# A sparse-attention and channel-mix kernel whose score matmuls write to PSUM in another order, with a re-ordered start

## Chip, cores and metric

The kernel runs on one core of one Trainium2 chip. The metric is the device time of one execution in microseconds. The kernel before took 571.46 us (median of three runs, 569.92 to 574.84).

## What is computed

Attention over 4 batches, 8 heads, 768 positions and a head size of 64. Positions lie in 24 blocks of 32. A query sees its own block and the neighbours, the first and the last block, and three sampled blocks; queries of the first and last block see everything. The attention's result is the input x of a channel mix with a gate:

```python
scores = scale * np.matmul(q, k.transpose(0, 1, 3, 2))
# mask: |blk_i - blk_j| <= 1, first and last block, sampled_blocks[qb]
attn = softmax(where(mask, scores, -1e9));  x = attn @ v     # as (B, S, 512)
x_prev = x shifted by one position
xk = mu_k * x + (1.0 - mu_k) * x_prev
xr = mu_r * x + (1.0 - mu_r) * x_prev
k = np.maximum(xk @ w_k, 0.0)
out = sigmoid(xr @ w_r) * (k * k @ w_v)
```

The weights arrive as 64-bit floats; q, k and v are 32-bit.

## The kernel before

**Attention** runs in 26 units (`all_units`, L266). Units 0 to 3 are wide: the first and last query block of one batch, against all 768 keys. Units 4 to 25 are near: one query block n = 1 to 22 of all four batches, against eight key blocks: three neighbours, the last or first block, and the block's own slots with the sampled blocks. A near unit (`near_unit`, L542) does two groups of head pairs. For each, 16 fp32 matmuls of 256 columns (L559) write scores `s`, DVE takes the maximum (L567), four exponentials on ACT write `p` (L539 in `direct_exp`), eight PE transposes and two copies turn it to `pt` (L523, L527 or L529), and 32 matmuls with the values give `o` (L585). `finish` (L648) divides, transposes (`tx`) and stores into `xt`.

A key slot holds values as (slot, head pair, position). The score matmul of L559 reads eight slots and writes them one after the other, so that a row of `s` is (c, slot, position). The values of a block of four slots lie in the partitions as (position, slot), so `p` has to be in the order (c, position, slot): L574 reads `s` as it lies, and the function `turned` (L576) writes `p` with a step of four values.

**The channel mix** goes over 12 tiles of 256 positions (`mixer`, L837): `split_x` makes xk and xr with their high and low parts (differences on POOL L740, mix on DVE L743, high part on ACT L750, low part on POOL L752), `gate` does r = xr w_r (L776), `hidden` h = xk w_k, relu and square (L794 to L811), `values` the product with w_v (L823). Each product is three matmuls: high-high, high-low, low-high.

**Weights** come in 20 blocks of 128 x 512 (`weight`, L358): blocks 0 to 3 are w_r, 4 to 11 w_k, 12 to 19 w_v. A block is 512 KB of 64-bit floats. ACT scales the upper words into `wmag` (L373), three DVE instructions make a 32-bit float `wf` (L378, L382, L386), then the high part is a copy (L396 on POOL for the blocks in `HI_POOL`, else L398 on ACT) and POOL subtracts it for the low part (L400). Blocks 0 to 11 are loaded into eight places of `early_w`, the others into `raw` tiles, which share four buffers with `p`.

**The sampled blocks** are looked up on the chip: `mask_setup` (L302) loads their numbers and a table of what is seen anyway, and `pack` (L310 to L336, 20 DVE instructions on one partition) replaces doubles by an empty block and packs six numbers into one word. SP reads that word before it issues the loads of sampled keys (L488) and values (L505) of each near unit.

**Order.** `plan.add(engine, ns, rank, ...)` lists every step with a cost and a due time (rank, in us). `Plan.order` (L190) goes through a model of the engines and picks for each engine, among the steps that can start soon, the one due first; the result is the fixed order of every engine's instructions. Costs and due times thus only set orders; the tables of due times stand at the end (L890 to L911). Each engine takes its instructions strictly in that order, and SP issues all loads and stores on one queue.

## Time and profile before

| | |
|---|---|
| runs | 571.46 us median (569.92, 571.46, 574.84) |
| profiled execution, its own time | 571.98 us |
| its span, first to last instruction | 570.2 us |
| mean granted clock of TensorE | 0.987 |
| busy: PE, ACT, POOL, DVE | 537.7, 325.2, 291.0, 269.6 us |
| bytes by DMA | 86.09 MB |
| chain that ended last, share of PE | 80% |

A row of the profile names the source line, engine, operation, output and input tile and the count; then busy time and the mean of one, and the idle time of the engine just before such instructions with what ended it. `<-` in a bracket names the instruction or transfer that was waited for. PE is the matmul stream and PEld its weight loads, which overlap it. An fp32 matmul counts as two matmul instructions with a weight load each, a transpose or a matmul of the mix as one. In the chain of waits a row is start, length, what, and how many instructions.

### The profile page before, as it was taken

The page shows a single profiled execution, that of the slowest core. Times are in us where ns is not written, and L with a number is a line of the kernel's source. Part 1 is how long each engine was busy: PE and PEld are TensorE (multiplying, and loading weights), DVE is VectorE, ACT ScalarE, POOL GpSimd, SP SyncE. Part 2 cuts the span into 40 slices and gives each one's busy share as a digit, 9 for nine tenths or more (in the row PEclk, how much of TensorE's full clock was granted, in tenths as well). Part 3 has the DMA queues.
Part 4 walks back from the last instruction along what each step waited for, and adds up shares of the span by engine and source line. Part 5 has one row for each costly group of instructions (what it writes and reads, how often), then busy time and mean ns, then how long its engine had stood idle before and what let it go on. Part 6 is the DMA issues. An engine that isn't in the chain of part 4 may idle for free.

```text
span 570.2 us, 18311 instructions
## 1 busy us (share of the span) xinstructions
PE 537.7 (94%) x7724; PEld 438.5 (77%) x7724; DVE 269.6 (47%) x533; ACT 325.2 (57%) x612; POOL 291.0 (51%) x359
## 2 busy tenths in 40 slices
PE   6788778979999999999999999999999999999997
PEld 2454556856887798897798798887877989889886
DVE  0877998887445353434424524433452242142411
ACT  0676687768478468467464756546564356424330
POOL 0430456887266066346066285373383663448752
PEclk9799899999999999999999999999999999999999
DMA  8999899773653553362651804135510302110001
GB/s 314 395 398 342 295 343 352 260 228 94 192 182 95 172 164 116 112 189 76 189 167 29 278 24 157 36 100 166 169 39 20 95 19 84 32 39 1 20 20 38
DMA packets 34183, 86.09 MB, mean 151 GB/s; under 512 B 5010, under 2 KB 5780, under 8 KB 31124
## 3 DMA queue, kind: packets, MB, share of 16 engines
q1 hardware_dynamic: 34100, 84.92, 44.5%
q8 instruction: 61, 1.00, 0.7%
q14 instruction: 22, 0.18, 0.1%
HBM read 78.60 MB, written 6.29 MB: 149 GB/s over the span
## 4 chain that ended last, share of the span: by engine, by line
PE 80%; DVE 9%; DMA 4%; ACT 2%; POOL 2%; issue 2%; SPq 0%; DVEq 0%; ACTq 0%
PE v L823 23%; PE o L585 6%; PE s L559 6%; PE t L523 6%; PE r_0p L776 5%; PE h_1p L794 5%; PE h_3p L794 5%; PE h_0p L794 5%; PE h_2p L794 5%; PE r_1p L776 4%; PE tw L523 2%; PE sw L608 2%; DVE nm L567 2%; PE tx L668 2%; DMA raw<-w_v 1%
## 5 line engine op out<-in xcount | busy, mean ns | idle before, releaser
L823 PE MATMUL v<-wv,k 128*128 128x512 f32 (+1 forms) x600 | 145.0, 391 | 0.0
L823 PEld LDWEIGHTS v<-wv,k 128*128 128x128 f32 x600 | 106.8, 188 | 22.8 <-DVE x L661 0.8
L539 ACT ACTIVATE p<-s,nm 128x256 f32<-128x256 f32 x176 | 104.1, 728 | 18.1 <-DVE nm L569 13.8
L567 DVE TENSOR_REDUCE nm<-s 128x4 f32<-128x1024 f32 x44 | 53.6, 1219 | 16.1 <-PE s L559 16.1
L523 PE MATMUL t<-ident,p 128*128 128x128 f32 x352 | 54.6, 278 | 4.7 <-ACT z L783 2.4
L585 PE MATMUL o<-VA,pt 128*32 128x65 f32 x2816 | 49.9, 222 | 6.7 <-ACT pt L527 4.0
L585 PEld LDWEIGHTS o<-VA,pt 128*32 128x32 f32 x2816 | 42.3, 109 | 16.9 <-issue 9.7
L752 POOL TENSOR_TENSOR xr<-xr_1f,xr 128x256 fp32r<-128x256 f32 x24 | 17.7, 737 | 70.8 <-ACT xr L750 70.8
L523 PEld LDWEIGHTS t<-ident,p 128*128 128x128 f32 x352 | 40.2, 140 | 16.1 <-ACT z L783 2.9
L527 ACT COPY pt<-t 128x512 f32<-128x512 f32 x68 | 40.7, 604 | 18.7 <-PE t L523 15.7
L559 PE MATMUL s<-KA,q 64*32 64x256 f32 x1408 | 46.5, 387 | 1.6 <-DVE wf L386 1.2
L743 DVE SCALAR_TENSOR_TENSOR xr_1f<-xr_1d,mk,xt 128x128 f32<-128x128 f32 x48 | 17.9, 372 | 55.9 <-POOL xr L752 46.3
L831 DVE SCALAR_TENSOR_TENSOR z<-v,z 128x512 f32<-128x512 f32 (+1 forms) x25 | 16.8, 670 | 50.1 <-PE v L823 50.0
L685 ACT COPY xt<-tx 128x512 f32<-128x512 f32 x22 | 13.0, 591 | 42.1 <-PE tx L668 42.0
L794 PE MATMUL h_0p<-xk,wk 128*128 128x256 f32 x288 | 37.0, 282 | 0.0
L776 PE MATMUL r_1p<-wr,xr 128*128 128x512 f32 x144 | 36.4, 400 | 0.6 <-ACT h_3k L807 0.6
L794 PE MATMUL h_3p<-xk,wk 128*128 128x256 f32 x288 | 36.4, 281 | 0.0
L743 DVE SCALAR_TENSOR_TENSOR xr_0f<-xr_0d,mk,xt 128x128 f32<-128x128 f32 x48 | 20.3, 424 | 34.0 <-POOL xk L752 13.9
L776 PE MATMUL r_0p<-wr,xr 128*128 128x512 f32 x144 | 36.4, 400 | 0.0
L794 PE MATMUL h_1p<-xk,wk 128*128 128x256 f32 x288 | 36.3, 281 | 0.0
L794 PE MATMUL h_2p<-xk,wk 128*128 128x256 f32 x288 | 36.3, 280 | 0.0
L794 PEld LDWEIGHTS h_0p<-xk,wk 128*128 128x128 f32 x288 | 35.1, 188 | 0.7
(139 smaller groups left out, 940.1 us busy)
## 6 DMA issues: line engine op xcount, KB each, us to landing
VA<-vt SPq DMA_DIRECT2D x93, 260.0 KB, 3.8
KA<-kt SPq DMA_DIRECT2D x90, 256.0 KB, 3.7
VA<-vw SPq DMA_DIRECT2D x24, 260.0 KB, 6.1
KA<-kq SPq DMA_DIRECT2D x16, 384.0 KB, 6.7
out<-z SPq DMA_DIRECT2D x23, 256.0 KB, 2.2
q<-qt SPq DMA_DIRECT2D x22, 256.0 KB, 4.3
early_w<-w_k SPq DMA_DIRECT2D x8, 512.0 KB, 6.4
raw<-w_v SPq DMA_DIRECT2D x8, 512.0 KB, 5.0
```

The costliest lines, as they stand in the source:

```text
L523: nc.tensor.transpose(tp.ap[:, i, :], p.ap[:, x : x + P], ident.ap)
L527: plan.add(ACT, 200 + 0.75 * P * many, rank + 0.1, lambda: nc.scalar.copy(pt.ap[:, 0:many], tp.ap[:, 0:many]), reads=[(tp,)], writes=[(pt,)])
L539: plan.add(ACT, 262 + 0.83 * width, rank, lambda: nc.scalar.activation(turned(p.ap[:, out]), view(), AF.Exp, bias=nm(), scale=SCALE), read ...
L559: nc.tensor.matmul(s.ap[ROWS[j], row, a * 256 : (a + 1) * 256].rearrange("p (n x) -> p n x", x=BLK), q.ap[half, (hp * QB + j) * BLK : (hp ...
L567: nc.vector.tensor_reduce(out=nm.ap.rearrange("p (r a) -> p r a", r=2), in_=s.ap.rearrange("p r (a x) -> p r a x", a=2), axis=AX.X, op=ALU ...
L585: nc.tensor.matmul(o[gi].ap[ROWS[j], i * DV : (i + 1) * DV], pts[row].ap[:, 2 * a + g, ROWS[j]], VA.ap[:, c0 + g, j, h * DV : (h + 1) * DV ...
L743: nc.vector.scalar_tensor_tensor(out=parts(f.ap[:, i, :]), in0=parts(d.ap), scalar=mk.ap[:, which, c : c + 1], in1=cols(c, 1), op0=ALU.mul ...
L752: plan.add(POOL, 80 + 2.4 * MIX * tw, rank + O_MIX, lambda f=f, cs=cs: nc.gpsimd.tensor_tensor(out=dst.ap[:, 1, cs], in0=f.ap, in1=dst.ap[ ...
L776: nc.tensor.matmul(pr.ap[:, 0:512], xr.ap[:, a, c, :], wr.ap[:, w, c, :], start=(c == 0 and m == 0), stop=(c == CC - 1 and m == 2))
L794: nc.tensor.matmul(ph.ap[:, ff * TT : (ff + 1) * TT], wk.ap[:, w, c, f * P : (f + 1) * P], xk.ap[:, a, c, :], start=(c == 0 and m == 0), s ...
L823: nc.tensor.matmul(pv.ap[:, 0:width], k2.ap[:, a, f, i * P : (i + 1) * P], wv.ap[:, w, f, cs], start=(f == 0 and m == 0), stop=(f == FC - ...
L831: plan.add(DVE, 150 + 1.05 * width, done, lambda pv=pv, cs=cs: nc.vector.scalar_tensor_tensor(out=z.ap[:, cs], in0=pv.ap[:, 0:width], scal ...
```

## The change

Four edits, and new tables of due times:

1. The score matmul writes its 256 columns in the order (c, position, slot), by a stepped output, and reads its eight key slots as before. `s` then lies as `p` has to, and the exponentials read and write 256 values that follow each other.
2. The due time of the sampled blocks' loads and of `pack` is -300 in place of -10.9 and -7.9, so both come first.
3. `HI_POOL` is 0 to 11 in place of 0 to 19: the high parts of the eight w_v blocks are copied on ACT (L398).
4. The planner's costs of `pack`, two weight instructions and the differences on POOL are changed.

```diff
-        plan.add(DVE, 4000, PICK + 3, pack, reads=[(number,), (con,)], writes=[(r,), (e,), (packed,)])
+        plan.add(DVE, 5500, PICK, pack, reads=[(number,), (con,)], writes=[(r,), (e,), (packed,)])
...
-            plan.add(DVE, 500, rank, shift, reads=[(mag,)], writes=[(mag,)])
+            plan.add(DVE, 600, rank, shift, reads=[(mag,)], writes=[(mag,)])
...
-            plan.add(DVE, 800, rank, tail, reads=[(mag,), (raw,)], writes=[(f,)])
+            plan.add(DVE, 930, rank, tail, reads=[(mag,), (raw,)], writes=[(f,)])
...
-    def direct_exp(p, out, s, view, nm, rank, key, turned=lambda x: x):
+    def direct_exp(p, out, s, view, nm, rank, key):
...
-            turned(p.ap[:, out]), view(), AF.Exp, bias=nm(), scale=SCALE), reads=[(s,), key[0]], writes=[(p, key[1])], table="exp")
+            p.ap[:, out], view(), AF.Exp, bias=nm(), scale=SCALE), reads=[(s,), key[0]], writes=[(p, key[1])], table="exp")
...
-                                s.ap[ROWS[j], row, a * 256 : (a + 1) * 256].rearrange("p (n x) -> p n x", x=BLK),
+                                s.ap[ROWS[j], row, a * 256 : (a + 1) * 256].rearrange("p (c x t) -> p c t x", c=2, t=QB),
...
-                                K[half, first : first + 2 * QB, j, xs], start=True, stop=True, skip_group_check=True)
+                                K[half, first : first + 2 * QB, j, xs].rearrange("p (c t) x -> p c t x", c=2), start=True, stop=True, skip_group_check=True)
...
-                direct_exp(p, slice(i * 256, (i + 1) * 256), s, lambda s=s, row=row, a=a: s.ap[:, row, a * 256 : (a + 1) * 256].rearrange("p (c j x) -> p c j x", c=2, j=QB),
-                           lambda nm=nm, i=i: nm.ap[:, i : i + 1], t1 + O_EXP[kind], ((nm,), i),
-                           lambda one: one.rearrange("p (c x j) -> p c j x", c=2, j=QB))
+                direct_exp(p, slice(i * 256, (i + 1) * 256), s, lambda s=s, row=row, a=a: s.ap[:, row, a * 256 : (a + 1) * 256],
+                           lambda nm=nm, i=i: nm.ap[:, i : i + 1], t1 + O_EXP[kind], ((nm,), i))
...
-        engine, ns, sub = (DVE, 70 + 1.04 * tw, nc.vector) if dve else (POOL, 80 + 2.07 * tw, nc.gpsimd)
+        engine, ns, sub = (DVE, 70 + 1.04 * tw, nc.vector) if dve else (POOL, 280 + 1.9 * tw, nc.gpsimd)
...
-HI_POOL = frozenset(range(20))
-
-PICK = -10.949
+HI_POOL = frozenset(range(12))
+
+PICK = -300.0
...
-UNIT_AT = [-9.20, 11.48, 39.66, 33.10, 52.53, 63.60, 71.98, 78.76, 95.46, 104.84, 132.94, 141.83, 159.00, 167.89, 184.38, 195.98, 213.06, 224.21, 284.51, 310.70, 320.53, 331.75, 388.52, 435.25, 445.15, 471.93]
+UNIT_AT = [-22.18, -27.40, -7.23, -18.64, 4.45, 12.07, 20.72, 26.61, 52.69, 67.00, 123.73, 130.36, 138.82, 146.33, 178.75, 187.42, 201.49, 212.32, 220.90, 269.30, 284.47, 293.08, 299.62, 341.83, 351.51, 457.85]
...
```

One line falls away above L576, so lines behind it have a number less by one in the changed kernel. Three places show how the instructions move.

**SP's queue at the start of the program.** `early_w` is a weight block, `q` a unit's queries, KA keys and VA values of the wide units; `number` and `con` are the two loads of the search. Before:

```order
L364 DMA early_w<-w_r 128x1024
L364 DMA early_w<-w_k 128x1024 x3
L461 DMA q_105<-qt 128x256
L467 DMA KA<-kq 128x768 x2
L461 DMA q_109<-qt 128x256
L467 DMA KA<-kq 128x768 x2
L364 DMA early_w<-w_r 128x1024
L471 DMA VA<-vw 128x520 x6
L467 DMA KA<-kq 128x768 x4
L471 DMA VA<-vw 128x520 x4
L461 DMA q_187<-qt 128x256
L471 DMA VA<-vw 128x520 x2
```

And now:

```order
L364 DMA early_w<-w_r 128x1024
L364 DMA early_w<-w_k 128x1024
L307 DMA number<-blocks 1x144
L308 DMA con<-seen 1x462
L364 DMA early_w<-w_k 128x1024 x2
L364 DMA early_w<-w_r 128x1024
L364 DMA early_w<-w_k 128x1024
L467 DMA KA<-kq 128x768 x2
L461 DMA q_135<-qt 128x256
L461 DMA q_137<-qt 128x256
L364 DMA early_w<-w_k 128x1024 x2
L467 DMA KA<-kq 128x768 x6
```

The search's loads, which stood behind the last row of the first list, are third and fourth now; six weight blocks in place of four, and a second unit's queries, stand ahead of the first unit that is computed (unit 1 now, unit 0 before). On DVE the 20 instructions of `pack` moved from behind the maxima of unit 3 to the very beginning.

**PE around the first values of tile 0.** `s9_1` are the scores of unit 9's second group, `o8_0` the values of unit 8's first, `t8_1_1` and the like transposes, `r0_1p` the gate and `v0_0_0` the first values product of tile 0. Before:

```order
L559 MATMUL s9_0_2146<-KA_67,q9_1717 32x256 x16
L776 MATMUL r0_1p_2168<-wr_72,xr0_1_1741 128x512 x6
L668 MATMUL tx7_2184<-ident_66,x7_2019 128x128 x4
L776 MATMUL r0_1p_2168<-wr_72,xr0_1_1741 128x512 x6
L523 MATMUL t8_1_0_2204<-ident_66,p8_1_2128 128x128 x4
L559 MATMUL s9_1_2210<-KA_67,q9_1717 32x256 x16
L585 MATMUL o8_0_2234<-VA_68,pt8_0_0_2123 32x65 x16
L585 MATMUL o8_0_2234<-VA_68,pt8_0_1_2166 32x65 x16
L523 MATMUL t8_1_1_2288<-ident_66,p8_1_2128 128x128 x4
L823 MATMUL v0_0_0_2294<-wv_1652,k20_1790 128x512 x9
L523 MATMUL t9_0_0_2319<-ident_66,p9_0_2202 128x128 x4
L823 MATMUL v0_0_0_2294<-wv_1652,k20_1790 128x512 x12
```

And now:

```order
L559 MATMUL s9_0_2106<-KA_67,q9_1721 32x2x4x32 x16
L793 MATMUL h0_3p_2127<-xk0_1668,wk_71 128x256 x24
L775 MATMUL r0_1p_2168<-wr_72,xr0_1_1896 128x512 x12
L822 MATMUL v0_0_0_2194<-wv_1335,k20_1904 128x512 x24
L822 MATMUL v0_1_0_2237<-wv_1335,k20_1904 128x512 x9
L523 MATMUL t8_0_0_2253<-ident_66,p8_0_2018 128x128 x4
L822 MATMUL v0_1_0_2237<-wv_1335,k20_1904 128x512 x6
L523 MATMUL t8_0_1_2269<-ident_66,p8_0_2018 128x128 x4
L822 MATMUL v0_1_0_2237<-wv_1335,k20_1904 128x512 x6
L523 MATMUL t8_1_0_2287<-ident_66,p8_1_2096 128x128 x4
L822 MATMUL v0_1_0_2237<-wv_1335,k20_1904 128x512 x3
L559 MATMUL s9_1_2299<-KA_67,q9_1721 32x2x4x32 x16
```

All 24 matmuls of `v0_0_0` now stand in one piece, ahead of unit 8's transposes, `s9_1` and `o8_0`. The shape of a score matmul's output reads 32x2x4x32 now, which is the stepped pattern.

**POOL where w_v is made.** `wv` are its high and low parts from `wf`, `xk0` and `xr0_1` parts of tile 0's inputs. Before:

```order
L396 CAST wv_1652<-wf16_1605 128x512
L400 TENSOR_TENSOR wv_1652<-wf16_1605,wv_1652 128x512
L740 TENSOR_TENSOR xr0_1d1_1713<-xt0_100 128x128
L740 TENSOR_TENSOR xr0_1d2_1739<-xt0_100 128x128
L752 TENSOR_TENSOR xr0_1_1741<-xr0_1f0_1676,xr0_1_1741 128x256
L740 TENSOR_TENSOR xr0_1d3_1775<-xt0_100 128x128
L396 CAST wv_1652<-wf14_1773 128x512
```

And now:

```order
L400 TENSOR_TENSOR wv_1335<-wf19_1759,wv_1335 128x512
L739 TENSOR_TENSOR xr0_1d1_1830<-xt0_100 128x128
L400 TENSOR_TENSOR wv_1335<-wf16_1803,wv_1335 128x512
L739 TENSOR_TENSOR xr0_1d2_1894<-xt0_100 128x128
L751 TENSOR_TENSOR xr0_1_1896<-xr0_1f0_1823,xr0_1_1896 128x256
```

The copies of L396 are gone from POOL here (they are CAST rows of L398 on ACT now), and blocks 12, 13 and 19 come before block 16, which was the first.

More of the change, by code (lines that the diff above doesn't have):

```diff
@@ L899 @@
 LAST = 10
-O_MAX, O_EXP, O_TR = [-122.23, 454.44, -1952.45, -530.44], [15.59, 118.13, -434.35, -150.84], [11.95, -1.08, 14.03, -664.60]
-O_PV, O_END = [-424.68, 28.50, -580.32, -554.50], [19.08, 16.82, 26.64, -48.33]
-SECOND = [-6.76, 5.49, -15.12, -7.04]
-LEAD_W, LEAD_Q, LEAD_K, LEAD_V = 31.394, 58.736, 95.899, 26.261
-O_MIX, O_SQ, O_SQ_FIRST = -34.483, 98.409, 4.566
-NEAR, STAY, STORE = 34.076, -1.502, 639.005
-UNIT_AT = [-9.20, 11.48, 39.66, 33.10, 52.53, 63.60, 71.98, 78.76, 95.46, 104.84, 132.94, 141.83, 159.00, 167.89, 184.38, 195.98, 213.06, 224.21, 284.51, 310.70, 320.53, 331.75, 388.52, 435.25, 445.15, 471.93]
-MIX_AT = [79.30, 115.80, 150.61, 177.85, 215.21, 285.90, 315.59, 371.74, 403.68, 439.62, 541.45, 890.68]
-MIX_RATE, MIX_RATE_LAST = 1.383, 22.393
-RAW_AT = [-36.24, -1206.10, 30.97, 34.27, -9.72, -484.29, 49.92, -566.15, -3.93, 47.41, 4.53, -311.04]
-WEIGHT_AT = [-568.38, -345.23, -12.43, 48.68, -219.95, -435.48, 77.39, 64.76, -260.14, 73.48, -151.20, 43.09, 88.08, 95.93, 81.50, 96.11, 79.73, 108.86, 92.25, 83.27]
+O_MAX, O_EXP, O_TR = [-136.60, 324.88, -2072.03, -180.71], [2.55, 744.56, -698.84, -627.94], [2.66, 3.53, 1.71, -1101.44]
+O_PV, O_END = [-651.62, 27.37, -915.04, -480.55], [13.00, 19.07, 18.19, -249.57]
+SECOND = [2.02, 2.74, -2.65, -47.38]
+LEAD_W, LEAD_Q, LEAD_K, LEAD_V = -6.619, 23.058, 602.922, -36.417
+O_MIX, O_SQ, O_SQ_FIRST = -189.083, 214.604, 3.569
+NEAR, STAY, STORE = 40.73, -8.683, 639.005
+UNIT_AT = [-22.18, -27.40, -7.23, -18.64, 4.45, 12.07, 20.72, 26.61, 52.69, 67.00, 123.73, 130.36, 138.82, 146.33, 178.75, 187.42, 201.49, 212.32, 220.90, 269.30, 284.47, 293.08, 299.62, 341.83, 351.51, 457.85]
+MIX_AT = [27.47, 61.12, 129.97, 168.02, 191.43, 216.25, 273.64, 298.57, 346.94, 436.67, 489.86, 707.12]
+MIX_RATE, MIX_RATE_LAST = 1.266, 9.119
+RAW_AT = [-178.23, -1100.74, 27.57, 30.95, -251.20, -110.49, 15.48, -956.21, -28.20, 1.82, -47.03, -207.39]
+WEIGHT_AT = [-355.42, -94.78, -68.65, -13.01, -222.24, -258.32, -83.94, -18.31, -176.00, 4.24, -106.66, -33.47, 8.92, 17.77, 34.64, 39.01, 28.49, 41.61, 29.54, 28.21]
 def kernel(**inputs):
```

## The prediction

> **What bounds the kernel now.** I read the page's engine shares, then busy time by stretch, then PE's waits and the chain of waits before the mixer's first values. From the page:
>
> ```profile
> PE 537.7 (94%) x7724; PEld 438.5 (77%) x7724; DVE 269.6 (47%) x533; ACT 325.2 (57%) x612; POOL 291.0 (51%) x359
> ...
> q8 instruction: 61, 1.00, 0.7%
> ```
>
> PE is the full engine. The stretches say where it is not full: 132.3 us is where the first values matmuls of tile 0 (`v0_0_0`) begin.
>
> ```profile
> 0.00:20.00 20.00, 12.90 (x52) 4.52 (x56) 5.47 (x9) 5.34 (x9) 2.67 (x9) 0.81 0.92 337
> 20.00:132.30 112.30, 93.94 (x2148) 66.91 (x2140) 96.59 (x178) 81.05 (x166) 63.47 (x66) 0.97 0.88 312
> 132.30:570.20 437.90, 430.87 (x5531) 367.08 (x5529) 167.51 (x348) 238.79 (x439) 224.88 (x285) 1.00 0.32 101
> ```
>
> Columns are the length, then busy us of PE, PEld, DVE, ACT, POOL, then the granted clock, the share of the DMA engines and GB/s. After 132.3 us PE idles 7.0 of 437.9 us. There a faster ACT or POOL buys nothing: the end is the start of `v0_0_0` plus PE's remaining work. Before it PE idles 7.1 + 18.4 us, while DVE is busy 96.6 of 112.3 us and the DMA engines 0.88. So the change is worth what it moves the start of `v0_0_0`, corrected for work that it moves across that point, plus whatever it does to PE's own durations.
>
> A second limit stands in this early stretch, PE's supply of instructions. The page's queue q8 loaded 1.00 MB in 61 packets, 16.4 KB each, and PE has 2 x 7724 instructions: about 253 to a packet. From PE's order of time:
>
> ```profile
> 29.08 1.11 PE L639 MATMUL o<-VA,ptw 128*32 128x65 f32 x64 [0.68 <-issue]
> ...
> 35.18 1.04 PE L639 MATMUL o<-VA,ptw 128*32 128x65 f32 x57 [1.01 <-issue]
> ```
>
> Twice it stops where it waits for nothing that is shown, 6.1 us apart, with 127 matmuls and as many weight loads between. That is a pace of about 42 per us; the stretch from 20 to 132.3 ran 4288 at 38.2 per us. PE's early part is not far from it.
>
> **The break-even.** In PE's order the change starts `v0_0_0` before the second scores of unit 9 (`s9_1`), `o8_0` and the four transposes of unit 8, which all stand ahead of it now. The pieces, from the chain of waits:
>
> ```profile
> 136.57 2.80 PE v L823 x12
> 139.37 0.44 PE t L523 x4
> 139.81 0.70 PE v L823 x3
> 140.51 1.05 PE o L585 x62
> ...
> 169.58 1.89 PE s L559 x64
> ```
>
> Scores of two groups take 1.89, so 0.95 + 1.05 + 4 x 0.44 = 3.8 us of work moves behind the mark. Against this stands one wait behind the mark now, which I take as gone since the whole block then runs unbroken:
>
> ```profile
> 132.33 2.34 PE L823 MATMUL v<-wv,k 128*128 128x512 f32 x9
> 135.91 0.66 PE L523 MATMUL t<-ident,p 128*128 128x128 f32 x4 [1.24 <-DVE pt L529]
> ```
>
> So `v0_0_0` must start by 132.3 - 3.8 + 1.2 = 129.7 us for no change of time.
>
> **The terms.** PE's waits from 44 to 133 us, in total, times, longest:
>
> ```profile
> PE o L585 <- ACT pt L527: 4.0, 2, 3.4
> PE o L639 <- ACT ptw L527: 2.4, 2, 2.2
> PE o L585 <- DMA VA<-vt: 1.6, 1, 1.6
> PE sw L608 <- ACT pw L539: 1.6, 2, 1.0
> PE s L559 <- DVE wf L386: 1.2, 1, 1.2
> PE tx L668 <- DVE x L661: 0.9, 1, 0.9
> PE o L585 <- issue: 0.8, 1, 0.8
> PE t L523 <- ACT xt L678: 0.7, 1, 0.7
> ```
>
> *Loads ahead of the first scores: +3.5.* Six weight blocks, two key loads and two queries now come ahead of PE's first scores, where four blocks, two key loads and one query did.
>
> ```profile
> 10.81 3.06 PE L608 MATMUL sw<-KA,q 64*64 64x384 f32 x16 [3.16 <-DMA KA<-kq]
> ```
>
> That is 6 x 512 + 2 x 384 + 2 x 128 = 4096 KB for 4 x 512 + 2 x 384 + 128 = 2944 KB, 1.18 MB more, at the first stretch's 337 GB/s 3.5 us. On ACT three more weight copies (`wmag`) stand ahead of the first exponentials, one of them behind a block that lands later still. The issues of the two small loads of the search stand ahead of these too. Bounds: 0, if the later wide units lose less than now, to +5.
>
> *The search among the sampled blocks moves into DVE's empty start: -3.4.* Its 20 instructions stand in the chain from
>
> ```profile
> 51.07 0.19 DVE pickf L316
> ...
> 55.86 0.04 DVE packed L336
> ```
>
> 4.9 us. They go to the time when the two small loads, third and fourth in SP's queue behind two blocks, have landed, well before the 10.8 us at which 2944 KB have, and DVE has nothing else then:
>
> ```profile
> 12.64 0.96 DVE L613 TENSOR_REDUCE nmw<-sw 128x2 f32<-128x768 f32 x1 [12.64 <-PE sw L608]
> ```
>
> Queued behind them on DVE is the first weight block only, whose own load lands later. If that cover were gone, the whole 4.9 us would stand before the first maxima. PE's waits that follow the search now are 2.2 for `ptw` and 1.2 for `wf`; I take these two, -3.4, between 0 (PE at its pace of instructions meanwhile) and -4.9. What is late next there is PE's supply.
>
> *Weights forward on DVE: -1.6.* Six blocks instead of three are converted by DVE's fourth wide maximum, and four instead of eight weight instructions are left when the first near scores come. I take PE's waits for `x` and `xt`, 0.9 + 0.7. Bounds: 0, and four instructions at the stretch's 96.59/178 = 0.54 us, -2.2.
>
> *First raw block of w_v earlier: -1.6.*
>
> ```profile
> 90.39 8.09 DMA raw<-w_v
> ```
>
> ACT waited here with four exponentials behind it. Now a block of w_v is issued between the queries of units 6 and its values' turn, about two units sooner, so this wait ends. PE lost little meanwhile, the 1.6 us for `VA<-vt`. The DMA engines at 0.88 cannot bring everything sooner; I take -1.6, between 0 and -8.1.
>
> *Eight high parts from POOL to ACT: -4.0, and exponentials: -1.0.*
>
> ```profile
> L539 ACT ACTIVATE p<-s,nm 128x256 f32<-128x256 f32 x176 | 104.1, 728 | 18.1 <-DVE nm L569 13.8 <-PE t L523 3.4 <-DVE wf L386 0.7
> ...
> L539 ACT ACTIVATE pw<-sw,nmw 128x384 f32<-128x384 f32 x32 | 16.0, 586 | 3.8 <-DVE pickf L316 2.6 <-DVE nmw L618 1.2
> ...
> L396 POOL CAST wv<-wf 128x512 fp32r<-128x512 f32 x8 | 5.2, 652 | 1.5 <-DVE wf L386 1.5
> ```
>
> POOL loses 8 x 0.652 = 5.2 us, all before `v0_0_0`. Its stretch of the chain is
>
> ```profile
> 113.41 0.76 POOL wv L396
> ...
> 118.55 0.68 ACT wmag L373
> ```
>
> and ends in PE's longest wait, 3.4 us for `pt` on ACT. I take both waits of that row, -4.0; bounds 0 and -5.2. The low part on POOL now waits for ACT's copy, which can stand behind a group of four exponentials, 2 us by the estimate below; behind it on POOL stand the mixer's next differences. POOL is busy 63 of these 112 us, which is the cover. ACT gains eight copies, some 0.6 each, and pays with the exponentials. Those write p with a step of four values now: 728 ns for 256 columns, where the wide ones, without a step, take 586 for 384. Without the step 256 columns lie between 586 x 256/384 = 391 and 586; I take 490, 0.24 us less, 42 us of ACT over 176. After 132.3 ACT has 199 us free, so only those early count; no row shows PE waiting more than a microsecond for them: -1.0, bounds 0 and -2.4.
>
> *TensorE's stepped write: 0.* The stride does not vanish, it moves from ACT's output to the matmul's. No matmul here writes with a step. The nearest rows: 32 score instructions in 0.95 us, eight tiles (64 by 32) at a time, make 0.92 ns per column, while 12 `v` in 2.80 us make 0.46 ns. PSUM is thus shown to accept contiguous columns twice as fast as the scores send them; a step that halved the acceptance would stay hidden. The other end is ACT's price, 0.24 us for 256, 0.95 ns per column: scores twice as long, 0.95 us a group, 44 groups, +42 us. I take 0, as the row of the same engine is nearer.
>
> The Trainium skill, "PSUM — Partial Sum Buffer", section "Specifications (TRN2)", says that PSUM has 8-byte cachelines and that any non-contiguous pattern slows matmuls significantly. That speaks against this change; by the sum above it would leave about 42 us more, and no run here shows it yet.
>
> *Later DIF costs, orders and due times* change no instruction. After the mark I count nothing, because PE stays full there; in the last 100 us the two orders end with the same 72 values.
>
> Sum: 132.3 + 3.5 - 3.4 - 1.6 - 1.6 - 4.0 - 1.0 = 124.2, against 129.7: 5.5 us earlier. The supply allows it: 4288 less the 224 instructions moved behind the mark, at 42 per us, is 96.8 us from 23.5, so 120.3. The profiled execution's span becomes 564.7, its own time 566.5. That execution lies 0.5 above the median of 571.46, so 571.5 - 5.5 = **566.0 us** is forecast.
>
> **Rivals.**
> *The step costs (slower).* Score groups grow at L559. For: ACT pays 0.24 us per 256 values for the same step. Against: half the write pace is unused. It decides from 5.5/44 = 0.13 us a group, where the gain is eaten; at 0.25 the kernel is slower by 1%; at the full 0.95 it takes 566 + 42 = 608 us. This is what the rule named above from the Trainium skill would do here.
> *The late start is not made up.* For: PE ran at 38.2 of 42 instructions per us, the wide part nearest to it, so relief on DVE and POOL shows little. With half of the 11.6 us credited, `v0_0_0` starts at 130.0: 571.8 us. With none, 135.8: 577.6.
> *More than forecast.* The pace of 6.1 us was seen with the DMA engines full; if it is 5% shorter, PE may start `v0_0_0` at 23.5 + 92.2 = 115.7, 14.0 us before break-even: 557.5. For: DVE's and POOL's loads both fall at once. Against: the DMA engines' 0.88.
> *The exponentials don't shorten*, if their 728 ns is not the step's: then ACT carries eight copies more and the last term is lost, 567 us; it stands inside the first two cases.
>
> **How the numbers follow.** Forecast, 561 to 570: 0.42. More: 0.18. Not made up: 0.22. The step costs: 0.18. A measurement tells about 1%, 5.7 us, from no change. The forecast lies on that edge: 0.27 of its 0.42 goes below 565.7, the rest within; more is all faster, 0.18. Not made up is within but for 0.02; of the step 0.17 is slower and 0.01 within. Faster 0.45, same 0.36, slower 0.19. The range, 557 to 577.6, goes from the shorter pace to no credit at all; it leaves out the full step and little else.
>
> **What would show it.** The near exponentials at some 490 ns; score groups still at 0.95 us (rival: up to 1.9); PE's first scores near 14.3 us; the search before 12 us; POOL without `wv` copies; `v0_0_0` at 124, and PE full behind it. A `v0_0_0` later than 129.7 with scores unchanged would make the forecast wrong, and so would new waits of PE after it.

## The result, and the profile after

The changed kernel takes 579.8 us (median of 15 runs, 575.1 to 582.8) against 572.7 us of the kernel before (15 runs, 569.9 to 574.8): 1.0122 times as long, 95% interval 1.010 to 1.0144. I had forecast 566.0 in a range up to 577.6. Its profiled execution took 582.16 us, 2.4 above its median; the span is 580.4. The two profiled executions differ by 10.2 us where the medians differ by 7.1, so a figure that is read from one trace alone can be off by some 3 us.

From the page of the changed kernel, the engines' shares and the two groups that the first edit touches:

```profile
PE 544.2 (94%) x7724; PEld 444.4 (77%) x7724; DVE 271.8 (47%) x533; ACT 303.1 (52%) x620; POOL 285.5 (49%) x351
...
L539 ACT ACTIVATE p<-s,nm 128x256 f32<-128x256 f32 x176 | 73.8, 480 | 26.9 <-DVE nm L569 24.2
...
L559 PE MATMUL s<-KA,q 64*32 64x256 f32 x1408 | 47.1, 382 | 5.0 <-issue 2.0
```

The first edit does what it says: the exponentials fall from 728 to 480 ns, and the scores, written with a step, are busy 47.1 us, where the page of before has

```profile
L559 PE MATMUL s<-KA,q 64*32 64x256 f32 x1408 | 46.5, 387 | 1.6 <-DVE wf L386 1.2
```

ACT is relieved by 22 us and POOL by 5.5. TensorE is busy 6.5 us longer with the same 7724 instructions. The busy time by stretch of the changed kernel, cut where `v0_0_0` begins (columns as in the prediction):

```profile
0.00:20.00 20.00, 9.41 (x36) 3.25 (x36) 10.75 (x29) 3.40 (x5) 4.11 (x11) 0.80 0.89 324
20.00:133.73 113.73, 94.78 (x2048) 67.10 (x2049) 87.32 (x157) 75.29 (x170) 54.18 (x55) 0.92 0.90 310
133.73:580.40 446.67, 440.05 (x5641) 374.06 (x5639) 173.74 (x349) 224.45 (x447) 227.20 (x287) 1.00 0.32 99
```

`v0_0_0` starts at 133.73, not at 124, and 4.0 us behind the break-even of 129.7. Behind the mark TensorE is busy 440.05 us against 430.87: 9.2 more, of which 3.8 were moved there. The forecast allowed nothing else. So there are two losses: one ahead of the mark, one behind it.

**The start.** TensorE's order of time in the changed kernel:

```profile
17.12 2.84 PE L607 MATMUL sw<-KA,q 64*64 64x384 f32 x16 [9.76 <-DMA q<-qt]
24.77 1.56 PE L607 MATMUL sw<-KA,q 64*64 64x384 f32 x8 [4.82 <-ACT pw L539]
...
33.02 1.56 PE L607 MATMUL sw<-KA,q 64*64 64x384 f32 x8 [3.10 <-ACT pw L539]
```

The first scores come at 17.1 us, 6.3 later than before, and wait for queries. (The traces of experiments 1, 5 and 8, with these loads in the same order, have them at 15.0 to 15.9 us, so they are 4 to 6 us late.) SP's queue shows why:

```profile
4.34 2.18 SPq L467 DMA_DIRECT2D KA<-kq  x2
6.57 1.33 SPq L461 DMA_DIRECT2D q<-qt  x2
```

The queries of the unit that is computed first (unit 1) are the second of these two, the twelfth load on the queue. Then the exponentials are late too. DVE between these first scores and the first exponentials:

```profile
18.75 0.94 DVE L612 TENSOR_REDUCE nmw<-sw 128x2 f32<-128x768 f32 x1
19.62 1.79 DVE L382 SCALAR_TENSOR_TENSOR wmag<-early_w,wmag 128x512 int32<-128x512 int32 x1
21.34 0.94 DVE L612 TENSOR_REDUCE nmw<-sw 128x2 f32<-128x768 f32 x1
22.20 0.67 DVE L386 SCALAR_TENSOR_TENSOR wf<-early_w,wmag 128x512 int32<-128x512 int32 x1
22.80 0.15 DVE L616 TENSOR_TENSOR nmw<-nmw 128x2 f32<-128x2 f32 x1
```

Two weight conversions stand between the two maxima and their combination, 2.5 us. ACT has a weight copy ahead of its first exponentials too, and that copy waits for the second of these conversions:

```profile
22.91 0.67 ACT L373 ACTIVATE wmag<-early_w 128x512 f32<-128x512 f32 x1 [1.92 <-DVE wf L386]
```

So both engines are ready for the first exponentials only at 23.6 us. And the granted clock (last column but two) stays low; ten microseconds each of the changed kernel, then of the kernel before:

```profile
20.00:30.00 10.00, 5.14 (x28) 2.20 (x28) 9.62 (x14) 4.72 (x10) 5.61 (x6) 0.56 1.03 400
30.00:40.00 10.00, 6.98 (x120) 4.19 (x121) 5.37 (x9) 4.32 (x10) 3.45 (x4) 0.66 0.87 284
```

```profile
20.00:30.00 10.00, 9.19 (x236) 6.12 (x228) 8.01 (x13) 6.39 (x14) 3.93 (x4) 0.87 1.04 396
30.00:40.00 10.00, 8.69 (x169) 5.29 (x157) 8.78 (x16) 7.17 (x16) 4.22 (x4) 1.00 1.03 399
```

In the trace the clock is halved from 11.8 to 28.9 and from 32.3 to 39.1 us, where before it is from 12.4 to 22.7.

To compare kernels I use **time lost**: time passed less the work done by then, each TensorE instruction counted at the pace that its kind has unbroken in the kernel before (a hidden matmul 0.114 us, gate and values 0.233, a score group 0.946, 64 near values 1.05, four transposes 0.43, eight wide scores 0.72, 96 wide values 1.5). The total is 508 us in every kernel. From the traces, in us:

| kernel | first scores | lost at 45 | at 70 | at 140 | at 550 | median |
|---|---|---|---|---|---|---|
| before | 10.8 | 24.2 | 34.1 | 51.4 | 64.1 | 572.7 |
| changed | 17.1 | 32.9 | 38.8 | 56.9 | 73.9 | 579.8 |

At 45 us the changed kernel is 8.7 behind, at 70 4.7, at 140 5.5, at the end 9.8. So the middle does give something back (4.0 between 45 and 70), much less than I credited, and 4.3 are lost where TensorE is full.

**Behind the mark** the waits are no worse. What differs is the pace. Two rows of the groups by line, before and then changed (mean ns of one at the end):

```profile
L794 PE MATMUL h_1p<-xk,wk 128*128 128x256 f32 x288 | 36.3, 281 | 0.0
```

```profile
L793 PE MATMUL h_1p<-xk,wk 128*128 128x256 f32 x288 | 37.5, 285 | 0.0
```

Measured from start to start of neighbours in one output tile (steps of 100 to 140 ns, some 1050 of them), a hidden matmul takes 115.5 ns before and 119.3 now; the most frequent step is 113 before and 120 now. Over 1152 that is 4.4 us. The gate (220 steps) goes the other way, 233.3 to 230.4 ns: 288 make 0.8 us. The values stay at 233.3 to 233.4.

Nothing in the diff names these matmuls. But their tiles lie elsewhere: a place is given to a tile when its kind is first used, and the search, now first, borrows the places of xr, xk and the like. In the built programs xk starts at byte 187968 of each partition before and at 152960 now, xr at 181696 and 142720; wk, wr, wv and k2 have not moved.

### The profile page after: what moved, and what is told of

Read it like the earlier page. It is cut to its first block, busy times and chain, and to the rows that moved or that the text cites. A ratio compares the mean times of both kernels' runs of the same rounds, so it can differ in the third digit from the quotient of the medians.

```text
span 580.4 us, 18318 instructions
## 1 busy us (share of the span) xinstructions
PE 544.2 (94%) x7724; PEld 444.4 (77%) x7724; DVE 271.8 (47%) x533; ACT 303.1 (52%) x620; POOL 285.5 (49%) x351
## 4 chain that ended last, share of the span: by engine, by line
PE 84%; DMA 6%; DVE 4%; ACT 2%; issue 2%; SPq 1%; POOL 1%; ACTq 0%
PE v L822 23%; PE o L584 7%; PE t L523 6%; PE s L559 6%; PE r_0p L775 6%; PE h_3p L793 6%; PE h_0p L793 6%; PE h_2p L793 6%; PE h_1p L793 5%; PE r_1p L775 5%; DMA VA<-vt 3%; PE o L638 2%; PE sw L607 2%; PE tw L523 2%; DMA early_w<-w_k 2%
## 5 line engine op out<-in xcount | busy, mean ns | idle before, releaser
L822 PEld LDWEIGHTS v<-wv,k 128*128 128x128 f32 x600 | 106.9, 188 | 25.7 <-POOL k L810 1.3
L539 ACT ACTIVATE p<-s,nm 128x256 f32<-128x256 f32 x176 | 73.8, 480 | 26.9 <-DVE nm L569 24.2
L567 DVE TENSOR_REDUCE nm<-s 128x4 f32<-128x1024 f32 x44 | 53.7, 1221 | 31.2 <-PE s L559 30.9
L559 PE MATMUL s<-KA,q 64*32 64x256 f32 x1408 | 47.1, 382 | 5.0 <-issue 2.0
L523 PEld LDWEIGHTS t<-ident,p 128*128 128x128 f32 x352 | 41.2, 142 | 11.8 <-issue 2.6
L739 POOL TENSOR_TENSOR xr_1d<-xt 128x128 f32<-128x128 f32 x48 | 19.9, 414 | 40.7 <-DVE xr_1f L742 29.1
L793 PE MATMUL h_3p<-xk,wk 128*128 128x256 f32 x288 | 38.1, 286 | 0.9 <-ACT h_2k L806 0.9
L739 POOL TENSOR_TENSOR xr_0d<-xt 128x128 f32<-128x128 f32 x48 | 19.7, 410 | 38.1 <-DVE xr_0f L742 21.2
L793 PE MATMUL h_2p<-xk,wk 128*128 128x256 f32 x288 | 37.6, 285 | 0.0
L793 PE MATMUL h_1p<-xk,wk 128*128 128x256 f32 x288 | 37.5, 285 | 0.0
L793 PEld LDWEIGHTS h_3p<-xk,wk 128*128 128x128 f32 x288 | 35.6, 191 | 2.0 <-ACT h_2k L806 1.4
L559 PEld LDWEIGHTS s<-KA,q 64*32 64x32 f32 x1408 | 23.9, 106 | 17.1 <-issue 5.3
```

The source lines that it names most:

```text
L523: nc.tensor.transpose(tp.ap[:, i, :], p.ap[:, x : x + P], ident.ap)
L539: plan.add(ACT, 262 + 0.83 * width, rank, lambda: nc.scalar.activation(p.ap[:, out], view(), AF.Exp, bias=nm(), scale=SCALE), reads=[(s,), ...
L559: nc.tensor.matmul(s.ap[ROWS[j], row, a * 256 : (a + 1) * 256].rearrange("p (c x t) -> p c t x", c=2, t=QB), q.ap[half, (hp * QB + j) * BL ...
L567: nc.vector.tensor_reduce(out=nm.ap.rearrange("p (r a) -> p r a", r=2), in_=s.ap.rearrange("p r (a x) -> p r a x", a=2), axis=AX.X, op=ALU ...
L739: sub.tensor_tensor(out=parts(d.ap), in0=cols(c, 0), in1=cols(c, 1), op=ALU.subtract)
L793: nc.tensor.matmul(ph.ap[:, ff * TT : (ff + 1) * TT], wk.ap[:, w, c, f * P : (f + 1) * P], xk.ap[:, a, c, :], start=(c == 0 and m == 0), s ...
```

## The experiments

**1. Places alone.** In each kernel the tiles are claimed in a fixed order ahead of the program; all instructions, orders and waits are unchanged.

```diff
+    for shape, dtype, tag, bufs in (...):      # the other kernel's order of tags
+        for k in range(bufs):
+            sb.tile(shape, dtype, tag=tag, bufs=bufs, name=f"lay_{tag}_{k}")
     for op in plan.order():
```

The changed kernel with the places of before:

> The changed kernel with the same instructions, order and waits, but with the work tiles (xk, xr, p, pt, kk, zr, q) at the SBUF places that they have in the kernel before. Theory A (places): the hidden matmuls' pace hangs on where xk lies; their spacing falls from 120 ns to mostly 113 to 118 ns, their busy sum from 151 to about 146 us, the gate goes from 227 back to 231 to 236 ns, and the time falls by 4 to 5 us to about 575. Rival B (order): the pace comes from how the new order strings the matmuls together; spacing stays at 120 ns and the time within 1.5 us of the changed kernel's. The start, first scores at 17 us and values of tile 0 at about 134 us, stays in both.

The kernel before with the places of the changed one:

> The kernel before with the same instructions, order and waits, but with the work tiles at the SBUF places that they have in the changed kernel. Theory A (places): hidden matmuls go from mostly 113 ns to 118 to 120 ns, the gate to 227 ns, and the time rises by 4 to 5 us to about 577. Rival B (order): spacing stays at 113 ns and the time within 1.5 us of 572.7.

Measured: 577.45 us for the first (ratio to before 1.0076, 1.005 to 1.0101), 574.89 for the second (1.0045, 1.0024 to 1.0066). The hidden step goes to 115.4 ns in the first and to 119.3 in the second, the gate's to 233.2 and 229.6. The rows, places of before in the changed kernel and places of the changed in the kernel before:

```profile
L793 PE MATMUL h_1p<-xk,wk 128*128 128x256 f32 x288 | 36.1, 280 | 0.0
```

```profile
L794 PE MATMUL h_1p<-xk,wk 128*128 128x256 f32 x288 | 37.5, 285 | 0.0
```

The pace goes with the places, whatever the order; theory B falls. In time it is 2.3 to 2.6 us, less than the 4 to 5 I expected, since the gate's gain goes off: 1152 x 3.9 ns - 288 x 3.7 ns = 3.4, inside the intervals. 4.9 of the 7.1 us stay when the places are put back.

**2. The first edit alone.** Its lines of the diff, in the kernel before.

> The kernel before with the stepped score write and the unturned exponentials alone; order, waits and places as before. Theory (the write is free, ACT's time is not what the path waits for): score groups stay at 0.95 us, near exponentials fall from 728 to about 480 ns, ACT's busy time falls by some 42 us, and the time falls by 0 to 2 us. Rival C (the early part waits for ACT): the values of tile 0 start 3 us or more sooner and the time falls by as much. Rival D (the step costs): score groups grow by 0.1 us or more and the time rises by 4 us or more.

Measured: 572.44 us, ratio 0.9995 (0.9975 to 1.0014). From its page:

```profile
PE 537.8 (94%) x7724; PEld 440.0 (77%) x7724; DVE 268.6 (47%) x533; ACT 299.6 (53%) x612; POOL 290.8 (51%) x359
...
L539 ACT ACTIVATE p<-s,nm 128x256 f32<-128x256 f32 x176 | 72.7, 481 | 18.0 <-DVE nm L569 14.2
...
L559 PE MATMUL s<-KA,q 64*32 64x256 f32 x1408 | 46.5, 386 | 2.6 <-DVE wmag L382 1.2
```

The scores are busy 46.5 us with the step as without. ACT's busy time falls by 25.6 us (42 were expected; exponentials overlap, and an overlap counts once), and the time does not move: what ACT saves here was not on the path.

**3. The search alone.** The three steps are moved by hand, the tiles stay in place.

```diff
+    ops = plan.order()
+    first = [op for op in ops if op.rank in (PICK, PICK + 3)]
+    rest = [op for op in ops if op not in first]
+    at = [i for i, op in enumerate(rest) if op.engine == SP][2]
+    for op in rest[:at] + first + rest[at:]:
```

> The kernel before, its tiles at the same places, with the search alone moved: its two small loads come third and fourth on the queue and its 20 instructions first on DVE; nothing else changes its place. As predicted (DVE's 4.9 us are on the path): PE's waits for the last turned copy and the first converted block, 2.2 and 1.2 us, go, the values of tile 0 start 3.4 us sooner, near 129, and the time falls by 3.4 us to about 569. Theory M (the transfers set when the values of tile 0 can start): the waits go or move to others, the start stays within 1.5 us of 132.3, and so does the time of 572.6.

Measured: 574.77 us, 1.0024 (1.0009 to 1.004): not faster. TensorE's waits between 44 and 136 us:

```profile
PE o L585 <- ACT pt L527: 3.4, 1, 3.4
PE o L585 <- DMA KA<-kt: 2.0, 1, 2.0
PE sw L608 <- ACT pw L539: 1.6, 2, 1.0
PE o L639 <- issue: 1.0, 1, 1.0
PE s L559 <- DVE wmag L378: 0.9, 1, 0.9
PE o L585 <- DMA VA<-vt: 0.7, 1, 0.7
PE o L639 <- ACT ptw L527: 0.7, 1, 0.7
```

Of the waits for `ptw` 0.7 is left in place of 2.4, and the 1.2 for `wf` is gone, nearly as forecast. New are 2.0 for keys and 0.9 for another weight block. Yet `v0_0_0` starts at 136.0, 3.6 us later than before. From 45 us to that start, in the kernel before and here:

```profile
45.00:132.33 87.33, 71.71 (x1642) 52.78 (x1640) 75.81 (x141) 64.36 (x131) 53.22 (x56) 0.98 0.84 289
45.00:135.96 90.96, 78.03 (x1650) 57.99 (x1643) 71.59 (x123) 65.20 (x132) 54.78 (x58) 0.89 0.82 284
```

TensorE idles 12.9 us here in place of 15.6, so waits did go. But it is busy 6.3 us longer with nearly the same number of matmuls, at a granted clock of 0.89 in place of 0.98: the clock is halved for 20.5 us of this stretch, against 3.4. What halves it is not shown, and over the seven runs a lower clock does not clearly go with a longer time (573.67 us at 0.976, 574.77 at 0.985). So the run shows that the term gave no gain, and that fewer waits did not bring the start forward; what took their place stays open.

**4. The copies alone.** `HI_POOL` of the changed kernel in the kernel before, places of before.

```diff
-HI_POOL = frozenset(range(20))
+HI_POOL = frozenset(range(12))
```

> The kernel before at its own places, with the high parts of the eight w_v blocks copied on ACT alone; ACT's and POOL's orders differ by these copies, the others' by nothing that counts. As predicted (POOL's stretch is on the path): PE's 3.4 us wait for the turned copy near 119 us goes, the values of tile 0 start 4 us sooner, the time falls by 4 us to 568.5. Rival (as with the search and the exponentials, another wait takes its place): the time stays within 1.5 us of 572.5.

Measured: 575.4 us, 1.0055 (1.0027 to 1.0083): slower. TensorE near 124 us, then ACT, POOL and DVE ahead of that:

```profile
123.71 1.03 PE L523 MATMUL t<-ident,p 128*128 128x128 f32 x4 [4.51 <-ACT p L539]
```

```profile
116.36 0.62 ACT L398 CAST wv<-wf 128x512 fp32r<-128x512 f32 x1 [2.09 <-DVE wf L386]
...
120.94 0.60 ACT L807 ACTIVATE h_3k<-h_3p 128x512 f32<-128x512 f32 x1 [1.76 <-POOL k L811]
...
122.42 0.62 ACT L398 CAST wv<-wf 128x512 fp32r<-128x512 f32 x1 [0.23 <-DVE wf L386]
122.94 1.20 ACT L539 ACTIVATE p<-s,nm 128x256 f32<-128x256 f32 x2
124.47 0.62 ACT L398 CAST wv<-wf 128x512 fp32r<-128x512 f32 x1 [0.33 <-DVE wf L386]
```

```profile
117.06 1.31 POOL L400 TENSOR_TENSOR wv<-wf,wv 128x512 fp32r<-128x512 f32 x1 [1.32 <-ACT wv L398]
```

```profile
117.49 0.90 DVE L569 TENSOR_SCALAR nm<-nm 128x4 f32<-128x4 f32 x1
```

The copy on ACT waits 2.1 us for DVE's converted block, POOL's low part 1.3 us for that copy, and ACT then 1.8 us for POOL's next result. The exponentials, whose maxima are there at 118.4 us, stand behind all this and a second copy and begin at 122.9. The 3.4 us for `pt` became 4.5 for `p`. Behind that wait the clock is halved from 124.4 to 131.2 us, and six gate matmuls take 2.93 us where the kernel before has 1.67; how much of the 3 us each of the two makes is not separated.

**5. Transfers.** Both kernels without the sampled loads of query blocks 3 to 6.

```diff
-            for j in range(NRAND):
+            for j in range(0 if n in (3, 4, 5, 6) else NRAND):
```

> The changed kernel without the loads of the sampled keys and values of query blocks 3 to 6 (it computes with older ones): 24 loads, 6.2 MB, 19.5 us of the transfers at 320 GB/s; the order of all engines is the same. Theory M (transfers): the values of tile 0 start 6 us or more sooner than 133.7, and the time falls by as much. Rival E (PE's supply of instructions, or DVE's work, sets the pace up to there): the start moves by less than 3 us.

> The kernel before without the same 24 loads. Theory M (transfers): the values of tile 0 start 6 us or more sooner than 132.3. Rival E (DVE is busy 97 of these 112 us, and sets the pace here): less than 3 us. If M holds for the changed kernel and E for this one, the change did free DVE, and the transfers kept the gain.

One run each. In the kernel before `v0_0_0` starts at 132.0 in place of 132.3, 571.25 us: the transfers do not set it, theory M falls there. In the changed kernel it starts at 128.6 in place of 133.7, 576.61 us. That is 5.1 for 19.5 us of transfers, between the two theories; and the twin of the changed kernel in experiment 1, whose program differs in places alone, has this start at 131.2, 2.5 sooner without any such cut. Inconclusive there.

**6. A late start alone.** Two weight blocks of the kernel before are loaded ahead of its first queries and keys; `new` gives the heads of the orders by index, all else stays.

```diff
+    new = {SP: [0, 1, 2, 3, 10, 30, 4, 5, 6, 7, 8, 9, *range(11, 30)]}
```

> The kernel before with two weight blocks (1.05 MB) loaded ahead of the first queries and keys, nothing else moved: the first scores come 3 to 4 us later than 10.8. Theory S (a late start is carried to the end): the time rises by 2.5 to 4 us, to 575 to 576.5. Theory M (the start is made up before the values of tile 0): within 1 us of 572.3.

Measured: 575.16 us, 1.0045 (1.0022 to 1.0067), 2.5 us more. TensorE's first scores:

```profile
13.59 3.73 PE L608 MATMUL sw<-KA,q 64*64 64x384 f32 x16 [6.46 <-DMA KA<-kq]
```

2.8 us late at the first scores, 2.5 us late at the end, as theory S has it. But the lateness is not simply carried. TensorE's order is the same in both kernels, so one can compare when the same instruction starts in the two traces: those that start at 36 us in the kernel before are 1.2 us late here, at 45 to 75 us 1.6 to 1.9, at 132 us 2.3 and at 550 us 3.2. More than half is made up at first, and lost again. And in the trace of experiment 2, with all loads in the order of the kernel before, the first scores happen to come 1.7 us later than in that kernel's trace, and at 36 us nothing of it is left (0.2 us ahead). So two blocks loaded first cost 2.5 us here; that a late first score as such reaches the end is not shown.

**7. Taking the late start out of the changed kernel.** First by the planner, with two blocks due later; then three times by hand.

```diff
-RAW_AT = [-178.23, -1100.74, 27.57, 30.95, -251.20, -110.49,
+RAW_AT = [-15, -1100.74, 27.57, 30.95, -251.20, -14,
```

> The changed kernel at the places of before, with the loads of two weight blocks due later (behind the first keys and queries), so that four blocks stand ahead of the first scores and no weight copy on ACT ahead of the first exponentials; the planner orders the rest. First scores come near 11 to 12 us in place of 17.1 and the clock is halved over less of the first 40 us. Theory S (the late start is carried to the end): of the 8.7 us that the changed kernel is behind at 45 us nearly all comes back, and the time falls by 4 us or more, from 577.5 to 573 or less. Theory M (the transfers set the start of the values of tile 0): these still start near 131 to 134 us and the time falls by less than 2 us.

```diff
+    new = {SP: [0, 1, 2, 3, 4, 5, 8, 9, 10, 11, 6, 7],
+           ACT: [6, 7, 8, 9, 0, 1, 2, 10, 11, 12, 13, 14, 15, 16, 3, 4, 5],
+           DVE: [0, 8, 10, 12, 1, 2, 3, 4, 5, 18, 6, 7, 9, 20, 11, 22, 13, 14, 15, 16, 17, 19, 21, 23, 24]}
```

> The changed kernel at the places of before, with its first instructions put by hand in another order and nothing else moved: the fifth and sixth weight block are loaded behind the first two keys and the two queries; on ACT the first four exponentials stand ahead of the first three weight copies, and the second unit's four ahead of the next three; on DVE the first unit's maxima stand ahead of the conversions. First scores come near 12 us, first exponentials near 17 in place of 23. Theory S (the late start is carried to the end): the time falls by 4 us or more, from 577.5 to 573.5 or less. Theory M (something later sets the start of the values of tile 0): it falls by less than 2 us.

```diff
+    new = {SP: [0, 1, 2, 3, 4, 5, 11, 8, 9, 10, 14, 15, 6, 7, 16, 17, 21, 24, 25, 26, 12, 18, 19, 13, 27, 28, 29, 20, 22, 23],
+           ACT: [6, 7, 8, 9, 0, 1, 10, 11, 12, 13, 14, 15, 16, 2, 17, 18, 19, 20, 21, 3, 22, 23, 24, 25, 26, 27, 4, 28, 29, 5],
+           DVE: [0, 8, 10, 12, 1, 2, 4, 18, 3, 5, 20, 7, 22, 6, 9, 11, 25, 26, 27, 13, 15, 17, 28, 29, 30, 31, 32, 14, 16, 19, ...]}
```

> A second order by hand for the start of the changed kernel (places of before), since the first one only moved the conversions ahead of the third unit's maxima. Now the queries of the unit that is computed first are loaded ahead of its keys, the first eight key loads and four value loads come before the seventh and eighth weight block, and the conversions stand one block between two units' maxima, as in the kernel before. First scores come near 11 to 12 us, first exponentials near 16, and the loss at 45 us (time less dense work) falls from 31.5 to about 25. Theory S (the late start is carried): the time falls by 4 us or more, from 577.5 to 573.5 or less. Theory M: by less than 2 us.

> A third order by hand for the start of the changed kernel (places of before). In the second, the activation table was loaded at 17.5 us in the way of the first exponentials, conversions still stood between the second unit's maxima, and TensorE's first values matmuls stood behind the third unit's scores. Now one block is converted ahead of the first scores, in time in which ACT and DVE wait for loads; the others stand one behind each later unit's maxima, on ACT and POOL too; the first values matmuls stand ahead of the third unit's scores. First scores near 12 us, first exponentials near 16 to 17, second unit's near 21, and the loss at 45 us falls from 31.5 to 25 to 27. Theory S (late start carried): the time falls by 3 us or more, from 577.5 to 574.5 or less. Theory M: less than 1.5 us.

> The same as the third order by hand, with xr at the place that it has in the changed kernel and xk at that of before. By the gain of the two places in the kernel before (2 us), 1.5 to 2.5 us less than the third order by hand at the places of before.

(The third order loads SP as the second; in it some weight blocks are converted when their place has been loaded anew, so the mix is done with other weights.) All four miss their aim: the loss at 45 us did not fall. From the traces:

| kernel | first scores | lost at 45 | at 70 | at 140 | at 550 | median |
|---|---|---|---|---|---|---|
| changed, places of before | 15.0 | 31.5 | 38.8 | 54.8 | 68.3 | 577.5 |
| first order by hand | 14.4 | 36.6 | 42.8 | 61.6 | 77.6 | 584.3 |
| second | 12.3 | 31.5 | 39.5 | 57.9 | 72.2 | 580.1 |
| third | 12.8 | 34.1 | 46.2 | 62.3 | 78.3 | 587.8 |
| by the planner | 14.8 | 32.6 | 45.3 | 73.8 | 88.1 | 595.5 |
| before, late by two blocks | 13.6 | 25.7 | 34.9 | 53.7 | 67.3 | 575.2 |

In the second order first scores are 2.7 us earlier and the gain is gone before 45 us. A row of its ACT shows one reason: the first instruction was now an exponential, and the table load that a weight copy drew at 0.7 us fell between the maxima and it.

```profile
17.46 1.28 ACT L539 ACT_TABLE_LOAD   x1 [17.46 <-DVE nmw L617]
```

The planner's order changed the middle as well and tells nothing of the start. The orders by hand change only the first instructions of the engines, and 4.0, 0.7 and 7.4 us more lost at 70 us are 9.3, 3.9 and 10.0 more at 550. Compared by the same instruction, as in experiment 6, the three are 6.6, 1.7 and 10.1 us late at 70 us, 9.2, 4.3 and 9.8 where `v0_0_0` starts, and 9.4, 4.0 and 10.0 at 550: what is late at the mark stays late. But these are no late starts. Their first scores come earlier than in the kernel that they were made from, and between 37 and 60 us TensorE waits 6.0, 5.3 and 7.0 us for ACT, where that kernel waits 0.7. The two runs of the third order, 587.81 and 587.45 us, do not tell their places apart (the gate's step is 233.1 and 229.2 ns, as its place has it).

**8. More warm-up.**

```diff
-            for i in range(times):
+            for i in range(times + 24):
```

> The changed kernel at the places of before, with 24 more warm-up matmuls ahead of its first scores (8 us, in time in which TensorE waits for the loads), nothing else moved. The granted clock then stays full some 7 us longer than 12.9 us. If the halved clock of the first 37 us is on the path, the time falls by 2 to 4 us to 574 or 575; if TensorE waits for exponentials there anyway, it stays within 1 us of 577.5.

Measured: 579.29 us (1.0112, 1.0064 to 1.016), no faster than 577.45; the intervals overlap. The edit missed its aim: the clock stayed full 1.3 us longer (halved from 14.2 us on in place of 12.9), not 7, and it was halved for 17.1 us in place of 20.5 of the first 40, which can be worth 1.7 us at most. The loss at 45 us is 30.8 in place of 31.5. Between 45 and 130 us TensorE then stops for 8.6 us where nothing is shown that it waits for (`issue`), against 0.3 in the kernel without the edit. So whether the halved clock of the start costs time of its own is not settled by this run.

**9. Which tile's place, and a faster kernel.** The kernel before with the first edit and other orders of the tiles.

> The kernel before with the stepped score write and unturned exponentials, and with xr at the place that it has in the changed kernel while xk stays where it is. If each product's pace goes by its own tile's place, the hidden matmuls stay at 113 to 118 ns, the gate's go from 231 to 236 ns to 227, 288 of them make 1 to 2 us, and the time falls by 1 to 2 us to about 571. If the gate's pace is set by something else that moved, the time stays within 0.7 us of 572.5.

> The kernel before with the stepped score write, xr at the changed kernel's place and xk at that of before (as in the best run so far), and k2, the stationary operand of the values matmuls, moved from byte 210880 to 146816 of each partition. If a product's pace goes by the places of its own two tiles, the values matmuls, 233.4 ns in every kernel so far with k2 and wv in one place, change for the first time, as the gate's did (by 3 to 4 ns either way), while hidden stays at 115.6 and gate at 229.5; 600 of them at 3.7 ns make 2.2 us, so the time goes to 568 or 572.5. If the pace goes by something else, 233.4 stays.

> The same kernel with k2 where it was and xk at a third place, byte 146816 (187968 gave 115.4 ns, 152960 gave 119.3). If the pace goes by the place of xk, the hidden matmuls change while gate and values stay; 1152 of them at up to 3.9 ns make up to 4.5 us either way, and the time 570 to 575. If 115.4 stays, it was not xk's own place.

| places (byte) | xk | hidden | xr | gate | k2 | values | median |
|---|---|---|---|---|---|---|---|
| of before, first edit | 187968 | 115.4 ns | 181696 | 233.3 ns | 210880 | 233.4 ns | 572.4 |
| xr moved | 187968 | 115.6 | 142720 | 229.5 | 210880 | 233.2 | 570.2 |
| and k2 moved | 187968 | 115.0 | 142720 | 228.8 | 146816 | 228.6 | 569.4 |
| xk moved, k2 not | 146816 | 119.4 | 142720 | 229.6 | 210880 | 233.3 | 574.2 |

Each product changed when the place of its own tile did, and only then. The row of the values in the kernel before and with k2 moved:

```profile
L823 PE MATMUL v<-wv,k 128*128 128x512 f32 x552 | 139.5, 400 | 0.0
```

```profile
L822 PE MATMUL v<-wv,k 128*128 128x512 f32 x552 | 136.9, 396 | 0.0
```

With xk moved the time rises by 4.0 us over the kernel with xr moved, where 1152 x 3.8 ns make 4.4. The kernel with xr and k2 moved takes 569.38 us, 0.994 of the kernel before (0.9917 to 0.9964), and beats both kernels; of its gain the part of k2 alone, 0.8 us by the medians, is not told apart from none, although 600 x 4.6 ns would make 2.8.

## Why the prediction was wrong, point by point

- **The sum.** It has a slip of its own: `v0_0_0` has 3.8 us less work ahead of it, which I put into the break-even but not into the start of 124.2. By its own terms the start would have been 120.4 and the gain 9.3 us, so the terms were even further off than 566.0 shows. The same slip stands in the rivals and in the upper end of the range: with no credit at all the start would have been 132.0 and the time 573.8, not 577.6.
- **Loads ahead of the first scores, +3.5.** Right in sign, too small: first scores 4 to 6 us later, and 8.7 us lost by 45 us. I counted bytes up to the first scores and not which load is last (the queries of the unit that is computed first), nor what the exponentials then stand behind. My bound of +5 named the weight copies on ACT; in the trace the last of them waits for DVE's conversions, which also stand between the maxima.
- **Weights forward on DVE, -1.6.** Two of the conversions that I put down as a gain are the rows at 19.62 and 22.20 above, ahead of the first exponentials. The waits for `x` and `xt` that I named are gone up to the mark. No run tested this term alone.
- **The search, -3.4.** It ran from 5.2 to 10.2 us, as said, and most of its two waits went. Alone it gave no gain (1.0024): TensorE idled less, and the start came later all the same.
- **The copies, -4.0.** Alone they cost 3 us (1.0055). The low part on POOL waits for ACT's copy, as I had named it (1.3 us); what I had not is that the copy itself waits for DVE, and that a group of exponentials stands behind it and begins 4.5 us after its maxima are there.
- **The exponentials, -1.0.** 480 ns, forecast 490; alone the time stays (0.9995).
- **First raw block sooner, -1.6.** TensorE's wait for `VA<-vt` fell from 1.6 to 0.6 up to the mark, but it is 3.6 in the same kernel with the places of before. No run tested it alone.
- **The stepped write, 0.** Right. The rule of the Trainium skill, "PSUM — Partial Sum Buffer", section "Specifications (TRN2)", that any non-contiguous pattern slows matmuls significantly, is not borne out by this pattern: 46.5 us with the step of four values and without. The scores send a column every 0.92 ns; whether a faster matmul would be slowed no run here shows.
- **Nothing behind the mark.** This step failed by 4.3 us. I had taken "the same instructions" for "the same time". The places of the tiles, which the moved search sets, were not among my cases, and they carry the result out of the range: without them it would be 577.5, just inside its upper end. That is luck, since the upper end has the slip in it.
- **The rivals.** The case that the late start is not made up came nearest (up to 577.6), in part by the slip. Two weight blocks loaded first cost 2.5 us without any of the other edits. The reason that I gave for this case, TensorE's supply of instructions, is neither shown nor excluded: stops for which nothing is shown make 4.9 us between 45 and 130 us in the changed kernel's trace, 0.8 in the kernel before, but 0.3 in the changed kernel with the places of before.

The failing step, in one sentence: I summed waits that end on DVE, POOL and ACT as if each one removed brought the start of `v0_0_0` forward by its length, and three runs with one part each took 1.4 (by the ratio) to 2.2 us more, 3.1 us more and the same time where I had credited gains of 3.4, 4.0 and 1.0. In the changed kernel itself, by the time lost, the start that I had put at +3.5 is 8.7 at 45 us, and of the 11.6 credited 3.2 are there at 140 us.

What stays open is what makes the 4.9 us left with the places put back. The late start fits: at 70 us that kernel has lost 4.7 more than the kernel before. But no order by hand took it away, and the copies (3.1 us alone) and the search (1.4 to 2.2) are rivals: no run took one of them out of the changed kernel. With the two blocks loaded first (2.5) these single costs come to 7 us or more, so they do not simply add up either.

## What to carry to other kernels

Where a re-ordering moves the start, follow the operand that lands last for the unit computed first, and what stands on every engine between it and the first result; two blocks loaded ahead of it cost 2.5 us at the end here. Waits in a stage where several engines take turns are not a sum: try each part alone, since a wait that is removed need not bring the next stage forward. Look at more than one trace of the same order before a wait of a microsecond or two is given a price, and compare where the tiles lie before pricing matmuls as unchanged.

## What the runs showed of the hardware

- The pace of one and the same matmul hangs on where its operand lies: hidden (moving xk) 115.0 to 116.1 ns at byte 187968, 119.3 at 152960, 119.4 at 146816; gate (stationary xr) 233.1 to 233.4 at 181696, 228.8 to 230.5 at 142720; values (stationary k2) 233.2 to 233.4 at 210880, 228.6 at 146816. What makes a place good is not known from these runs. The Trainium skill, "TensorE: Matmul & The Clock Gate", section "Wait — 56ns, not 53.3ns?", gives the step of back-to-back matmuls as the columns at 2.4 GHz and about 2.5 ns more, without regard to the place; for 256 columns that makes an estimate of 109.2 ns. The runs differ: the most frequent steps here, with a weight load for each matmul, are 113 and 120 ns.
- The granted clock has only full and half, in pieces that are multiples of 3.41 us: up to 560 us halved for 10.2 and 3.4 us in the kernel before, for 17.1, 6.8 and 3.4 in the changed one. It differs between traces of one order: the kernel before has 13.7 us in all, kernels that differ from it in places or the first edit alone have 17.1 to 23.9.
- An output step of four values costs ACT 0.25 us per 256 values (728 to 481 ns alone). The same step in TensorE's write to PSUM costs the scores nothing that shows (46.5 us busy with it and without, a column every 0.92 ns).
